# Gates of two hidden-layer units computed as Exp, add, reciprocal and product instead of Silu

## The chip, the cores and the metric

The program runs on one core of a Trainium2 chip. The time is the device time of one execution in microseconds (us); 678.58 us is the median of three runs (678.49 to 678.67). Engines are named as in the profile: PE multiplies matrices (PEld loads its weights), DVE is the vector engine, ACT the scalar engine that evaluates functions from tables, POOL the general engine, SP the queue that starts most transfers.

## The reference

Attention with a sliding window and sink keys, then two feed-forward layers, all in float32. Inputs are 2 batches of 768 tokens, 8 heads of 64, so 1536 tokens of width 512.

```python
scores = scale * np.matmul(q, k.transpose(0, 1, 3, 2))      # q, k, v: (2, 8, 768, 64)
keep = is_sink | in_window                                  # 4 sink keys, window 128
a = np.exp(scores - max);  a = a / (sum(a) + 1e-09);  x = a @ v
g = x @ w_gate                                              # (1536, 512) @ (512, 1536)
silu = g * (1.0 / (1.0 + np.exp(-g)))
y = (silu * (x @ w_val)) @ w_out
h = y @ w_in                                                # 512 -> 2048
out = (np.maximum(h, 0) + alpha * np.minimum(h, 0)) @ w_out2
```

## The kernel before

Tokens are cut into three passes of 512 (`b` = 0, 1, 2). Every float32 product is made of three matmuls of split operands (high by high, low by high, high by low), so a 128x512 projection tile is 12 matmuls (L613 to L615). Weights come as 64-bit numbers; a `Stream` turns them into high and low halves: a copy on ACT (L520), three DVE steps (`w_m`: L536, L539, L542), a copy `wh` on ACT (L550) and a subtraction `wl` (L557, on POOL during attention, on DVE later).

**Attention.** 24 groups of two query blocks and two heads go through a software pipeline (`attention`, L322). In step x group x gets its scores (PE L217; DVE L221 and L223; ACT Exp into `pr`, L227), group x-1 its normalisation (DVE L243 and L244, POOL L259 and L260), group x-3 its product with v (PE L313 and L316 into `xp`; ACT `xh` L805; DVE `xl` L806) and group x-2 its transposes (PE L272, L295; ACT L283, L296; POOL L284, L288).

**Two units woven in.** Once the 512 tokens of a pass are through attention, the first unit of the first layer for that pass, `m1.unit(0, b)`, is taken up piece by piece between attention's steps (`product`, L819). That happens for `b` = 0 and `b` = 1; the third pass and all later chunks run behind attention in `mix`. A unit has four hidden tiles, in two pairs: two gate projections `pg`, a gate `sg` for each (L656, L657), two value projections `pv`, the product `hid` (DVE L665), its halves `hh` (ACT L626) and `hl` (DVE L627). Then the four tiles go through the output projection `po`.

**What sets the order.** During attention the DVE instructions stand in the order in which the program writes them (`manual_schedule`, L799); on the other engines a scheduler sets the order when the program is built. Each engine then runs its list in order. All PSUM tiles, `pg` among them, come from one pool of eight buffers (L865), so a new tile waits until an earlier one has been read for the last time.

**Tables.** [...] Before an Exp (L227) that follows a Silu (L657), and before a Silu that follows an Exp, the built program holds an ACT_TABLE_LOAD. Copy and Abs need none here.

Of the kernel before, what the change touches and what calls it, by code (L numbers as in the profile page):

```python
# [11 lines left out]
AF = mybir.ActivationFunctionType  # L12
ALU = mybir.AluOpType
# [459 lines left out]
def new_acc(g, name):  # L473
    for pool in g.acc_ps:
        if pool[1]:
            pool[1] -= 1
            return pool[0].tile([P, KD, T], F32, tag="acc", name=name), pool
    assert False


def big(g, dt, name):
    return g.x_p.tile([P, KD, T], dt, tag="x", name=name)
# [126 lines left out]
def proj(nc, ps, w, xh, xl):  # L609
    wh, wl = w  # L610
    for kk in range(KD):
        c = slice(kk * P, (kk + 1) * P)
        nc.tensor.matmul(ps, wh[:, c], xh[:, kk], start=(kk == 0), stop=False)  # L613
        nc.tensor.matmul(ps, wh[:, c], xl[:, kk], start=False, stop=False)  # L614
        nc.tensor.matmul(ps, wl[:, c], xh[:, kk], start=False, stop=(kk == KD - 1))  # L615
# [5 lines left out]
def hidden_pair(g):  # L621
    return [g.h_p.tile([P, 2, T], F32R, tag=t, name=t) for t in ("hh", "hl")]


def split_hidden(nc, hid, hh, hl):
    nc.scalar.activation(hh, hid, AF.Copy)  # L626
    nc.vector.tensor_tensor(out=hl, in0=hid, in1=hh, op=ALU.subtract)  # L627


class Moe1:  # L630
# [4 lines left out]
    def unit(self, c, b):  # L635
        nc, g, st = self.nc, self.g, self.st
        nch = NF1 // CHUNK
        w0 = self.base + c * 3 * CHUNK

        def at(kind, x):  # L640
            return w0 + 2 * (x - x % 2) + 2 * kind + x % 2

        xh, xl = self.xs[b]
        last = b == len(self.xs) - 1
        hid_of = []
        for x in range(0, CHUNK, 2):
            pair = hidden_pair(g)
            pss, sgs = [], []
            for r in range(2):
                ps = g.ps_m.tile([P, 512], F32, tag="ps", name="pg")  # L650
                proj(nc, ps, st.get(at(0, x + r)), xh, xl)
                pss.append(ps)
                if r == 0:
                    yield
            for ps in pss:
                sg = g.t_p.tile([P, T], F32, tag="sg", name="sg")  # L656
                nc.scalar.activation(sg, ps, AF.Silu)  # L657
                sgs.append(sg)
            yield
            for r in range(2):  # L660
                hh, hl = (t[:, r] for t in pair)
                ps = g.ps_m.tile([P, 512], F32, tag="ps", name="pv")
                proj(nc, ps, st.get(at(1, x + r)), xh, xl)
                hid = g.t_p.tile([P, T], F32, tag="hid", name="hid")
                nc.vector.tensor_tensor(out=hid, in0=ps, in1=sgs[r], op=ALU.mult)  # L665
                split_hidden(nc, hid, hh, hl)
                hid_of.append((hh, hl))
                if last and r == 1:
                    st.done(4)
                yield  # L670
        if c == 0:
            self.accs[b] = new_acc(g, "acc1")
        acc, home = self.accs[b]
        if c == nch - 1:
            yh, yl = big(g, F32R, "yh"), big(g, F32R, "yl")
        for m in range(KD):
            mc = slice(m * P, (m + 1) * P)
            ps = g.ps_m.tile([P, 512], F32, tag="ps", name="po")
            for x, (hh, hl) in enumerate(hid_of):
                wh, wl = st.get(w0 + 2 * CHUNK + x)  # L680
                nc.tensor.matmul(ps, wh[:, mc], hh, start=(x == 0), stop=False)  # L681
                nc.tensor.matmul(ps, wl[:, mc], hh, start=False, stop=False)  # L682
                nc.tensor.matmul(ps, wh[:, mc], hl, start=False, stop=(x == CHUNK - 1))  # L683
            av = acc[:, m]
            if c == 0:
                nc.scalar.activation(av, ps, AF.Copy)
            else:
                nc.vector.tensor_tensor(out=av, in0=ps, in1=av, op=ALU.add)
            if c == nch - 1:
                split_hidden(nc, av, yh[:, m], yl[:, m])  # L690
            yield
        if c == nch - 1:
            home[1] += 1
            self.put(yh, yl)
        if last:
            st.done(CHUNK)
# [241 lines left out]
```

## Time and profile before

| | |
|---|---|
| median of 3 runs | 678.58 us |
| the profiled execution | 679.03 us, span 677.3 us |
| PE busy | 656.8 us, 97% of the span |
| DVE busy | 395.5 us, 58% |
| ACT busy | 297.4 us, 44% |
| POOL busy | 82.7 us, 12% |
| mean granted PE clock | 0.983 of full speed |

The span is what the profiler saw; the execution's own time is 1.7 us longer. The page cuts the span into 40 slices of 16.9 us and gives the busy share of each engine and the granted PE clock in tenths. In a list of groups each line has the busy time, the mean duration of one instruction, and the idle time of the engine in front of it with the instruction that ended it. In a timeline a bracket after a row is idle time of that engine just before the row, and what ended it. The first unit that is woven in has its gates at 57 to 85 us, the second at 127 to 155 us; the last Exp of attention is at 163 us.

### The profile page before, as it was taken

Reading aid. Unit: us, or ns where it says so; the run is one execution under the profiler, and the core shown is the slowest. Engines: PE = TensorE matmul, PEld = TensorE weight load, DVE = VectorE, ACT = ScalarE, POOL = GpSimd, SP = SyncE. Lnnn points to the kernel's source line nnn. Section 1 sums busy time; section 2 is a strip of 40 time slices with the busy share of each in tenths; the row PEclk is TensorE's granted clock in tenths of the full one; section 3 lists DMA queues with packets and bytes.
Section 4 is the critical chain, followed back from the end, with each engine's and each line's share of the span. In section 5 each row is a group of like instructions: output and inputs, shape, how many; then the busy total and the mean of one; then the engine's idle time right before and its main releaser. Section 6 shows DMA issues by size and latency. Waiting matters only on the chain.

```text
span 677.3 us, 8596 instructions
## 1 busy us (share of the span) xinstructions
PE 656.8 (97%) x3098; PEld 520.0 (77%) x3098; DVE 395.5 (58%) x880; ACT 297.4 (44%) x680; POOL 82.7 (12%) x137
## 2 busy tenths in 40 slices
PE   7789899999999999999999999999999999999996
PEld 4457566767788888888888888888888888888885
DVE  6997867353389923389332789419734744334332
ACT  4767756765476612255221546336522333112320
POOL 3557544334100000000000000000000000000000
PEclk8969799999999999999999999999999999999999
DMA  8854444100055510045200134203400000000111
GB/s 274 259 158 136 146 135 145 31 13 1 1 180 168 180 63 1 4 124 180 65 1 0 39 118 133 84 1 95 154 1 0 1 1 0 1 0 8 55 63 67
DMA packets 37203, 52.29 MB, mean 77 GB/s; under 512 B 4384, under 2 KB 28960, under 8 KB 37152
## 3 DMA queue, kind: packets, MB, share of 16 engines
q1 hardware_dynamic: 34944, 51.65, 24.0%
q8 instruction: 26, 0.43, 0.3%
q10 hardware_dynamic: 2208, 0.01, 0.2%
q14 instruction: 25, 0.20, 0.1%
HBM read 48.51 MB, written 3.15 MB: 76 GB/s over the span
## 4 chain that ended last, share of the span: by engine, by line
PE 86%; DVE 6%; ACT 3%; DMA 1%; issue 1%; POOL 1%; SPq 0%; ACTq 0%; POOLq 0%
PE ph L613 6%; PE ph L615 6%; PE pf L739 6%; PE pf L737 6%; PE pf L738 6%; PE ph L614 6%; PE po L681 5%; PE po L682 5%; PE po L683 5%; PE pv L613 5%; PE pv L615 5%; PE pv L614 5%; PE pg L613 5%; PE pg L614 4%; PE pg L615 4%; PE ps_s L217 2%
## 5 line engine op out<-in xcount | busy, mean ns | idle before, releaser
L626 ACT ACTIVATE hh<-hid 128x512 fp32r<-128x512 f32 x84 | 53.0, 632 | 69.6 <-DVE hid L665 40.2
L627 DVE TENSOR_TENSOR hl<-hid,hh 128x512 fp32r<-128x512 f32 x84 | 58.2, 693 | 35.8 <-ACT hh L626 35.6
L613 PE MATMUL ph<-yh,wh 128*128 128x512 f32 x192 | 74.8, 390 | 0.0
L615 PE MATMUL ph<-yh,wl 128*128 128x512 f32 x192 | 74.8, 389 | 0.0
L738 PE MATMUL pf<-wl,hh 128*128 128x512 f32 x192 | 74.7, 389 | 0.0
L614 PE MATMUL ph<-yl,wh 128*128 128x512 f32 x192 | 74.7, 389 | 0.0
L737 PE MATMUL pf<-wh,hh 128*128 128x512 f32 x192 | 74.7, 389 | 0.0
L719 ACT ACTIVATE neg<-ph,sal 128x512 f32<-128x512 f32 x48 | 33.0, 687 | 93.0 <-PE ph L615 93.0
L739 PE MATMUL pf<-wh,hl 128*128 128x512 f32 x192 | 72.1, 389 | 0.0
L550 ACT ACTIVATE wh<-w_m 128x512 fp32r<-128x512 f32 x68 | 42.6, 630 | 64.6 <-DVE w_m L542 23.4
L721 DVE SCALAR_TENSOR_TENSOR hid<-ph,sig,neg 128x512 f32<-128x512 f32 x48 | 36.0, 750 | 38.2 <-ACT neg L719 38.0
L613 PE MATMUL pg<-xh,wh 128*128 128x512 f32 x144 | 57.9, 403 | 0.0
L613 PE MATMUL pv<-xh,wh 128*128 128x512 f32 x144 | 56.9, 395 | 0.3 <-ACT pt L283 0.3
L614 PE MATMUL pg<-xl,wh 128*128 128x512 f32 x144 | 57.2, 397 | 0.0
L615 PE MATMUL pg<-xh,wl 128*128 128x512 f32 x144 | 56.9, 395 | 0.0
L681 PE MATMUL po<-hh,wh 128*128 128x512 f32 x144 | 56.6, 395 | 0.2 <-ACT pr L227 0.2
L615 PE MATMUL pv<-xh,wl 128*128 128x512 f32 x144 | 56.1, 390 | 0.0
L614 PE MATMUL pv<-xl,wh 128*128 128x512 f32 x144 | 56.1, 389 | 0.0
L682 PE MATMUL po<-hh,wl 128*128 128x512 f32 x144 | 55.9, 390 | 0.0
L557 DVE TENSOR_TENSOR wl<-w_m,wh 128x512 fp32r<-128x512 f32 x56 | 38.3, 688 | 27.9 <-ACT wh L550 27.9
L744 DVE TENSOR_TENSOR acc<-pf,acc 128x512 f32<-128x512 f32 x36 | 23.2, 686 | 52.0 <-PE pf L739 52.0
L683 PE MATMUL po<-hl,wh 128*128 128x512 f32 x144 | 52.9, 390 | 0.0
(106 smaller groups left out, 1203.8 us busy)
## 6 DMA issues: line engine op xcount, KB each, us to landing
w_raw<-in_moe_w_out SPq DMA_DIRECT2D x28, 512.0 KB, 3.5
w_raw<-in_moe_w_in SPq DMA_DIRECT2D x16, 512.0 KB, 3.8
w_raw<-in_moe_w_gate SPq DMA_DIRECT2D x12, 512.0 KB, 4.4
w_raw<-in_moe_w_val SPq DMA_DIRECT2D x12, 512.0 KB, 3.9
th<-in_qk SPq DMA_DIRECT2D x16, 336.0 KB, 3.3
vr<-in_v SPq DMA_DIRECT2D x16, 192.0 KB, 2.6
out<-acc SPq DMA_DIRECT2D x12, 256.0 KB, 2.2
th<-in_qk SPq DMA_DIRECT2D x8, 256.0 KB, 5.3
```

The costliest lines, as they stand in the source:

```text
L550: nc.scalar.activation(wh, m, AF.Copy)
L613: nc.tensor.matmul(ps, wh[:, c], xh[:, kk], start=(kk == 0), stop=False)
L614: nc.tensor.matmul(ps, wh[:, c], xl[:, kk], start=False, stop=False)
L615: nc.tensor.matmul(ps, wl[:, c], xh[:, kk], start=False, stop=(kk == KD - 1))
L626: nc.scalar.activation(hh, hid, AF.Copy)
L627: nc.vector.tensor_tensor(out=hl, in0=hid, in1=hh, op=ALU.subtract)
L681: nc.tensor.matmul(ps, wh[:, mc], hh, start=(x == 0), stop=False)
L682: nc.tensor.matmul(ps, wl[:, mc], hh, start=False, stop=False)
L683: nc.tensor.matmul(ps, wh[:, mc], hl, start=False, stop=(x == CHUNK - 1))
L737: nc.tensor.matmul(ps, hh[:, ts], wh, start=(x == 0), stop=False)
L738: nc.tensor.matmul(ps, hh[:, ts], wl, start=False, stop=False)
L739: nc.tensor.matmul(ps, hl[:, ts], wh, start=False, stop=(x == CHUNK - 1))
```

## The change

For the first chunk (`c == 0`) of the first two passes (`b < 2`), which are the two units woven into attention, the gate g * 1/(1 + exp(-g)) is written out: Exp with scale -1 on ACT, then on DVE an addition of 1, a reciprocal and the product with `pg`. All other gates keep Silu. Eight gates change, four in each unit. Lines behind L657 move down by six.

```diff
             for ps in pss:
                 sg = g.t_p.tile([P, T], F32, tag="sg", name="sg")
-                nc.scalar.activation(sg, ps, AF.Silu)
+                if c == 0 and b < 2:
+                    nc.scalar.activation(sg, ps, AF.Exp, scale=-1.0)
+                    nc.vector.tensor_scalar(out=sg, in0=sg, scalar1=1.0, scalar2=None, op0=ALU.add)
+                    nc.vector.reciprocal(out=sg, in_=sg)
+                    nc.vector.tensor_tensor(out=sg, in0=ps, in1=sg, op=ALU.mult)
+                else:
+                    nc.scalar.activation(sg, ps, AF.Silu)
                 sgs.append(sg)
```

On DVE this is the list around the first pair of gates (at 55 us of the trace), before:

```order
177 L243 TENSOR_SCALAR rinv<-ssum 128x4
178 L244 RECIPROCAL rinv<-rinv 128x4
179 L536 TENSOR_SCALAR w_m<-w_m 128x512
180 L539 SCALAR_TENSOR_TENSOR w_m<-w_raw,w_m 128x512
181 L542 SCALAR_TENSOR_TENSOR w_m<-w_raw,w_m 128x512
182 L806 TENSOR_TENSOR xl<-xp,xh 128x256
183 L221 COPY_PREDICATED ps_s<-above,ps_s 128x128
```

The same place in the changed kernel's DVE list:

```order
177 L243 TENSOR_SCALAR rinv<-ssum 128x4
178 L244 RECIPROCAL rinv<-rinv 128x4
179 L659 TENSOR_SCALAR sg<-sg 128x512
180 L660 RECIPROCAL sg<-sg 128x512
181 L661 TENSOR_TENSOR sg<-pg,sg 128x512
182 L659 TENSOR_SCALAR sg<-sg 128x512
183 L660 RECIPROCAL sg<-sg 128x512
184 L661 TENSOR_TENSOR sg<-pg,sg 128x512
185 L536 TENSOR_SCALAR w_m<-w_m 128x512
186 L539 SCALAR_TENSOR_TENSOR w_m<-w_raw,w_m 128x512
187 L542 SCALAR_TENSOR_TENSOR w_m<-w_raw,w_m 128x512
188 L812 TENSOR_TENSOR xl<-xp,xh 128x256
```

The six gate steps stand ahead of a weight's conversion, of `xl` and of the next group's scores. The other three pairs are inserted in the same way, each right behind a normalisation; the rest of the DVE list in attention stays, but for a few neighbours that change places.

On ACT, at the same pair, before:

```order
60 L227 ACTIVATE pr,ssum<-ps_s,nb 128x160
61 L657 ACT_TABLE_LOAD
62 L657 ACTIVATE sg<-pg 128x512 x2
63 L550 ACTIVATE wh<-w_m 128x512
64 L805 ACTIVATE xh<-xp 128x256
65 L283 ACTIVATE pt<-ps_p 128x2x128 x2
66 L296 ACTIVATE pts<-ps_p_792 128x128
67 L520 ACTIVATE w_m,wsum<-w_raw 128x512
68 L227 ACT_TABLE_LOAD
69 L227 ACTIVATE pr,ssum<-ps_s,nb 128x160 x4
```

And after:

```order
60 L227 ACTIVATE pr,ssum<-ps_s,nb 128x160
61 L658 ACTIVATE sg<-pg 128x512 x2
62 L811 ACTIVATE xh<-xp 128x256
63 L283 ACTIVATE pt<-ps_p 128x2x128 x2
64 L296 ACTIVATE pts<-ps_p_798 128x128
65 L811 ACTIVATE xh<-xp 128x256
66 L283 ACTIVATE pt<-ps_p 128x2x128 x2
67 L550 ACTIVATE wh<-w_m 128x512
```

Both loads are gone, `xh` moves up and `wh` moves down behind the next group's copies. In the part of the list that runs with these inputs 16 loads become two: one for the first Exp and one for the first Silu behind attention.

The PE list keeps the order of its blocks (projections, scores, products, transposes). What changes is what they wait for. Between the two value projections of the first pair, with the semaphores waited for in brackets, before:

```order
163 L272 MATMUL ps_p<-ident,pr 128x128 [waits Activation_49]
164 L272 MATMUL ps_p<-ident,pr 128x128
165 L272 MATMUL ps_p<-ident,pr 128x128 [waits Activation_49]
166 L313 MATMUL xp<-pt,vr 64x128 [waits Pool_49]
167 L313 MATMUL xp<-pt,vr 64x128
168 L316 MATMUL xp<-pts,vsr 128x128 x2
169 L272 MATMUL ps_p<-ident,pr 128x128
170 L295 MATMUL ps_p_881<-ident,sk 128x128 [waits Activation_49]
171 L613 MATMUL pv<-xh,wh 128x512 [waits Activation_49]
```

And after:

```order
163 L313 MATMUL xp<-pt,vr 64x128 [waits Pool_49]
164 L313 MATMUL xp<-pt,vr 64x128
165 L316 MATMUL xp<-pts,vsr 128x128 x2
166 L272 MATMUL ps_p<-ident,pr 128x128 [waits DVE_49]
167 L272 MATMUL ps_p<-ident,pr 128x128
168 L272 MATMUL ps_p<-ident,pr 128x128 [waits Activation_49]
169 L272 MATMUL ps_p<-ident,pr 128x128
170 L295 MATMUL ps_p_887<-ident,sk 128x128 [waits Activation_49]
171 L613 MATMUL pv<-xh,wh 128x512 [waits DVE_49]
```

The transposes at row 166 take over the buffer of the pair's second `pg`, which is now read last by DVE's product (L661) and no longer by ACT; the projection at row 171 takes the buffer of the `xp` behind it and waits for DVE's `xl`.

## Rows read from the trace of the kernel before

**Rows 1.** The page: busy time of PE and DVE, the PE slices, the granted clock.
```profile
PE 656.8 (97%) x3098; PEld 520.0 (77%) x3098; DVE 395.5 (58%) x880; ACT 297.4 (44%) x680; POOL 82.7 (12%) x137
...
PE   7789899999999999999999999999999999999996
...
PEclk8969799999999999999999999999999999999999
```

**Rows 2.** Windows: length, busy time by engine (instructions), granted clock, DMA share, GB/s.
```profile
55.10:103.10 48.00, 44.08 (x243) 30.59 (x241) 36.15 (x100) 32.32 (x88) 26.05 (x36) 0.93 0.47 147
79.00:91.00 12.00, 12.00 (x55) 8.35 (x54) 5.55 (x12) 8.24 (x22) 6.39 (x10) 0.78 0.45 141
103.10:126.40 23.30, 23.09 (x128) 16.51 (x129) 14.49 (x64) 13.92 (x50) 10.46 (x19) 1.00 0.31 104
126.40:162.00 35.60, 34.77 (x202) 25.03 (x202) 15.76 (x66) 24.75 (x59) 11.52 (x24) 1.00 0.04 12
```

**Rows 3.** Groups of ACT: table loads and gates; busy us, mean ns, idle before.
```profile
L657 ACT ACTIVATE sg<-pg 128x512 f32<-128x512 f32 x36 | 21.2, 594 | 37.5 <-PE pg L615 37.4
...
L227 ACT ACT_TABLE_LOAD x8 | 10.3, 1283 | 3.7 <-DVE nb L223 1.9 <-PEq L922 1.7
L657 ACT ACT_TABLE_LOAD x8 | 10.3, 1283 | 0.1
```

**Rows 4.** Timeline of PE from 74 to 88 us: start, us, engine, instruction, idle before.
```profile
74.32 0.33 PE L295 MATMUL ps_p<-ident,sk 128*128 128x128 f32 x1 [0.37 <-ACT sg L657]
76.11 1.54 PE L217 MATMUL ps_s<-th 64*128 64x288 f32 x6 [1.47 <-ACT pr L227]
78.05 1.33 PE L217 MATMUL ps_s<-th 64*128 64x288 f32 x2 [0.40 <-ACT pt L283]
...
79.90 0.63 PE L614 MATMUL pg<-xl,wh 128*128 128x512 f32 x1
80.33 0.63 PE L615 MATMUL pg<-xh,wl 128*128 128x512 f32 x1
...
87.41 0.39 PE L615 MATMUL pv<-xh,wl 128*128 128x512 f32 x1
87.64 0.40 PE L613 MATMUL pv<-xh,wh 128*128 128x512 f32 x1
```

**Rows 5.** Timeline of ACT and DVE around the first two gates.
```profile
55.03 0.18 DVE L244 RECIPROCAL rinv<-rinv 128x4 f32<-128x4 f32 x1
...
55.95 1.28 ACT L657 ACT_TABLE_LOAD   x1
...
59.16 0.42 DVE L806 TENSOR_TENSOR xl<-xp,xh 128x256 fp32r<-128x256 f32 x1 [1.38 <-ACT xh L805]
```

**Rows 6.** Waits of DVE from 55.1 to 103.1 us: total us, times, longest.
```profile
DVE xl L806 <- ACT xh L805: 5.7, 2, 4.3
DVE hl L627 <- ACT hh L626: 2.9, 3, 1.3
DVE hid L665 <- PE pv L615: 1.8, 2, 1.6
```

**Rows 7.** Groups of DVE: the kinds of operation that the change adds, at several sizes.
```profile
L665 DVE TENSOR_TENSOR hid<-pv,sg 128x512 f32<-128x512 f32 x36 | 24.7, 687 | 44.7 <-PE pv L615 43.6 <-ACT sg L657 1.0
...
L531 DVE TENSOR_SCALAR w_m<-w_m 128x512 f32<-128x512 f32 x16 | 6.8, 423 | 0.7 <-ACT w_m L518 0.6
...
L100 DVE TENSOR_TENSOR sal<-alpha,sig 128x16 f32<-128x16 f32 x1 | 0.2, 175 | 0.0
...
L144 DVE TENSOR_SCALAR red<-lim_v 128x1 f32<-128x1 f32 x1 | 0.1, 143 | 0.0
```

**Rows 8.** The reciprocal's own line: duration in ns, least, median and greatest.
```profile
L244 DVE RECIPROCAL rinv<-rinv x24: 169/178/179, 10.5 to 165.2; 128x4 f32<-128x4 f32 x24
```

**Rows 9.** Timeline of DVE and PE at 69 us, and where both meet again.
```profile
69.16 0.74 DVE L627 TENSOR_TENSOR hl<-hid,hh 128x512 fp32r<-128x512 f32 x1 [0.70 <-ACT hh L626]
...
103.14 0.42 DVE L806 TENSOR_TENSOR xl<-xp,xh 128x256 fp32r<-128x256 f32 x1
...
103.61 0.44 PE L272 MATMUL ps_p<-ident,pr 128*128 128x128 f32 x2
```

**Rows 10.** Timeline of PE in the second unit: its only wait.
```profile
148.81 0.75 PE L217 MATMUL ps_s<-th 64*128 64x288 f32 x2 [0.83 <-ACT pr L227]
```

**Rows 11.** Waits of DVE from 126.4 to 162 us.
```profile
DVE xl L806 <- ACT xh L805: 11.9, 3, 5.7
DVE hid L665 <- PE pv L615: 5.2, 3, 2.5
```

## The prediction

> **What bounds the kernel now.** I read the page first: PE is busy 656.8 of 677.3 us, and its slices show that what it loses lies in the first sixth of the span, where the granted clock is also below full [rows 1]. Behind attention every slice is 9, so the change, which adds nothing there, can move the time only through the attention stage. Next I read that stage by windows around the two units woven in [rows 2]. From 55.10 to 103.10 us (48.00 us, the first unit's gates) PE is busy 44.08 us at a clock of 0.93, and DVE 36.15 us. From 126.40 to 162.00 us (35.60 us, the second unit's gates) PE is busy 34.77 us at full clock, DVE only 15.76 us. So the first unit sits where PE and DVE are both near full, the second where PE alone bounds.
>
> Then the groups of ACT show the price of alternating functions: 8 loads before a Silu and 8 before an Exp, 1283 ns each, 20.6 us in all [rows 3]. The timeline shows what part of that reaches PE. [...] In the second unit a load costs PE one wait of 0.83 us [rows 10]. Last I read DVE's waits in the first unit: 5.7 us for `xh`, late behind a load, 2.9 us for `hh`, 1.8 us for `pv` [rows 6].
>
> **The change part by part.**
>
> *Loads on ACT.* Sixteen become two; 14 x 1.283 = 18.0 us of ACT work goes. The eight Exp take the place of eight Silu of the same shape, 0.594 us [rows 3]; Exp itself at 128x512 is not in the trace, and I take the same. ACT bounds nothing for long (32.32 of 48.00 us in the first unit [rows 2]), so this is worth only what PE and DVE waited: on PE 0.37 + 1.47 + 0.40 = 2.24 us and the low clock behind it, twelve matmuls x (0.43 - 0.23) = 2.4 us [rows 4], and 0.83 us in the second unit [rows 10]; 5.5 us at the very best.
>
> *Three DVE steps for each of eight gates.* The addition is like the 128x512 TENSOR_SCALAR on float32 at L531, 0.423 us; the product from PSUM is like `hid`, 0.687 us [rows 7]. The reciprocal of 128x512 is not in the trace; that of 128x4 takes 178 ns [rows 8]. The nearest rows to scale it with are TENSOR_TENSOR at 16 and 512 elements, 175 and 687 ns [rows 7]: (687 - 175)/496 = 1.03 ns per element and a fixed part of 175 - 16 x 1.03 = 158 ns. Four elements at that rate would take 162 ns. The reciprocal takes 178, so (178 - 158)/4 = 5 ns per element, and 512 elements take 0.158 + 512 x 0.005 = 2.7 us. The lower bound is the ordinary rate, 0.69 us, if the 16 ns more are only a longer fixed part. The upper bound takes the fixed part from the one-element row, 143 ns [rows 7]: 35/4 = 8.75 ns per element, 4.6 us. I take 2.7 us, because it rests on the rows closest to it in kind. A gate then costs DVE 0.42 + 2.7 + 0.69 = 3.8 us, four gates 15.2 us.
>
> *What is queued behind them.* DVE runs in written order. In the first pair the gates stand ahead of a weight's conversion, `xl` and the next scores. DVE is free at 55.03 + 0.18 = 55.21 us; Exp can start where the load started, at 55.95 [rows 5], and ends 0.6 us later, so DVE first waits 1.35 us. The second pair stands behind scores and a normalisation; by then PE has its `pg` ready, and I count no wait. PE's transposes, products and `pv` now wait for L661 and for the `xl` behind it. Scores on ACT and POOL's normalisation move with DVE. The DMA queues get nothing new: the conversion that is pushed back belongs to weights that are needed two blocks later.
>
> *The sum for the first unit.* In the 48.00 us DVE has 36.15 us of work [rows 2]. Added: 15.2 us for the gates. Waits that remain: 1.35 us for the first Exp and three times 0.70 us, which is what `hl` waits for `hh` with no load in the way [rows 9], 2.1 us. The waits for `xh` and `pv` [rows 6] go, because DVE is now the late one. 36.15 + 15.2 + 1.35 + 2.1 = 54.8 us, 6.8 us more than 48.00. PE can't run ahead of that: at 103.61 us it starts transposes directly behind DVE's `xl` of 103.14 [rows 9], and after 103.10 DVE has little slack until PE bounds again (PE 23.09 of 23.30 us [rows 2]). So PE arrives 6.8 us later. Its own old waits and the low clock lie inside those 54.8 us and give nothing back. PE will now idle more in this stretch, and the rows show a low clock after such waits [rows 4]; where that falls at the end of the stretch it costs PE time, 2.4 us a time. I take half of one, 1.2 us.
>
> *The second unit.* Four gates are 15.2 us of DVE; DVE is idle 35.60 - 15.76 = 19.8 us there [rows 2], 11.9 us of it waiting for `xh` and 5.2 us for `pv` [rows 11]. This cover holds them, and PE's wait of 0.83 us goes: -0.8 us. If the reciprocal took 4.6 us, four gates would be 22.9 us and 3.1 us would show.
>
> *Together:* 679.03 + 6.8 + 1.2 - 0.8 = 686.2 us for an execution like the profiled one. That one lies 0.45 us above the median of 678.58, so 685.8 us.
>
> **The rivals.**
>
> *The reciprocal is slower still.* For: the four-element row allows 8.75 ns per element. Against: with the fixed part of the tensor operations it allows 5. At 4.6 us a gate costs 5.7 us, the first unit 36.15 + 22.9 + 3.45 = 62.5 us, 14.5 us more; the second unit shows 3.1 - 0.8 us more; 695.4 us against the median. [...] I give this rival 0.15.
>
> *The clock falls more.* Each further stretch at the lower level that ends in PE's own time costs 2.4 us [rows 4]; two more give 690 to 691 us. Chance 0.10.
>
> *Faster: the loads were what held PE, and DVE keeps up.* If the reciprocal runs at the ordinary rate of 0.69 us, a gate is 1.8 us, and the first unit takes 36.15 + 7.2 + 3.45 = 46.8 us, 1.2 us less than before; with the second unit's 0.83 us that is 676.6 us. If PE is then held by nothing it reaches -5.5 us, 673.1 us. The point from which this decides: four gates must cost less than 48.00 - 36.15 - 3.45 = 8.4 us, a reciprocal below 1.0 us. For it: the loads' waits are real [rows 4]. [...] Against it: the 178 ns. Chance 0.16.
>
> *No change.* A reciprocal between 1.0 and 1.7 us, or the two groups of lag in attention's pipeline, swallow the delay. The lag would do so only if PE had other work ready, but PE's list is fixed and waits for DVE's `xl` in it. Chance 0.12.
>
> **How the numbers follow.** The forecast itself, a delay of DVE in the first unit at 2 to 3.6 us per reciprocal, has 0.47, and its own range is 682 to 690 us. With the slower reciprocal and the lower clock, slower has 0.47 + 0.15 + 0.10 = 0.72. What counts as no change is 0.2% or 1.4 us, about what a measurement of this kernel can tell: 677.2 to 679.9 us, 0.12. Faster has 0.16. The range that should hold 8 of 10 goes from 676.2 us, which takes in the ordinary-rate case, to 696 us, the upper bound of the reciprocal; left out are the full 5.5 us gain below, and more clock loss on top of the upper bound.
>
> **What would show it.** Two table loads instead of sixteen, and none between 55 and 160 us. RECIPROCAL at L660: 2.7 us; under 1 us or over 4 us would make the forecast wrong by its step. In the first unit DVE busy nearly throughout, with no wait for `xh`, and its stretch from the norm ahead of the first gate to the `xl` that stood at 103.14 us some 55 us long. PE with new waits for L661 (`sg`), for `xl` (L812) and for `pr`, in place of those for ACT between loads. In the second unit PE without a wait for `sg`. If the stretch is longer by the gates' 15 us, the old waits were not there to be filled; if PE waits in the second unit too, its cover was read too generously.

## The result, and the profile after

The changed kernel takes 688.10 us (median of 4 runs, 687.07 to 689.14) against 678.62 us of the kernel before; the ratio is 1.014, with an interval of 1.0127 to 1.0153. It is slower by some 9.5 us. The forecast was 685.8 us, slower, in a range of 676.2 to 696.0.

The page of the changed kernel, answering to [rows 1]: busy time, PE's slices, the granted clock.

```profile
PE 660.7 (96%) x3098; PEld 521.7 (76%) x3098; DVE 426.3 (62%) x904; ACT 280.7 (41%) x666; POOL 83.0 (12%) x137
...
PE   7878988999999999999999999999999999999996
...
PEclk8889897999999999999999999999999999999998
```

ACT has 16.7 us less to do, DVE 30.8 us more, and PE's losses still lie in the first sixth of the span. The groups of the gates' steps answer to [rows 3, 7, 8] (busy us, mean ns, idle before):

```profile
L660 DVE RECIPROCAL sg<-sg 128x512 f32<-128x512 f32 x8 | 26.8, 3353 | 0.3
...
L661 DVE TENSOR_TENSOR sg<-pg,sg 128x512 f32<-128x512 f32 x8 | 5.5, 691 | 0.3
L658 ACT ACTIVATE sg<-pg 128x512 f32<-128x512 f32 x8 | 4.6, 595 | 2.2 <-PE pg L615 2.2
...
L659 DVE TENSOR_SCALAR sg<-sg 128x512 f32<-128x512 f32 x8 | 4.2, 530 | 1.6 <-ACT sg L658 1.6
L227 ACT ACT_TABLE_LOAD x1 | 1.3, 1283 | 1.7 <-PEq L928 1.7
L663 ACT ACT_TABLE_LOAD x1 | 1.3, 1283 | 0.0
```

Two loads are left of sixteen. Exp takes what Silu took (595 and 594 ns a gate). The reciprocal takes 3.353 us every time.

To see where the time went I cut both traces at the same three instructions, so that the same work lies between them: L244's norm ahead of the first gate, the fifth norm behind it (the first unit's gates lie between these), and the first `pg` behind attention. The windows of before (length, busy time by engine, clock, DMA share, GB/s):

```profile
55.03:106.10 51.07, 46.94 (x256) 32.67 (x255) 39.05 (x115) 35.17 (x98) 28.18 (x40) 0.93 0.49 152
106.10:181.24 75.14, 74.31 (x440) 53.97 (x438) 30.99 (x124) 43.77 (x123) 27.06 (x56) 1.00 0.09 29
```

And of the changed kernel:

```profile
55.62:115.42 59.80, 50.36 (x256) 34.73 (x255) 54.44 (x128) 28.28 (x92) 26.77 (x37) 0.86 0.40 126
115.42:191.32 75.90, 75.16 (x444) 54.30 (x442) 48.34 (x136) 33.89 (x115) 28.79 (x58) 1.00 0.10 29
```

Of the profiled difference of 10.0 us (span 687.3 against 677.3), 0.6 us is there at the first norm, ahead of every changed instruction. That is the spread of runs: in the profiles below this norm lies anywhere from 53.8 to 55.9 us, so I compare lengths from there. The first unit is 8.7 us longer, the rest of attention 0.8 us, and nothing is added behind it. In the first unit DVE is busy 54.44 of 59.80 us. Its timeline answers to [rows 5] (start, us, engine, instruction, idle before):

```profile
57.16 0.47 DVE L659 TENSOR_SCALAR sg<-sg 128x512 f32<-128x512 f32 x1 [1.35 <-ACT sg L658]
57.66 3.35 DVE L660 RECIPROCAL sg<-sg 128x512 f32<-128x512 f32 x1
61.05 0.69 DVE L661 TENSOR_TENSOR sg<-pg,sg 128x512 f32<-128x512 f32 x1
61.66 0.42 DVE L659 TENSOR_SCALAR sg<-sg 128x512 f32<-128x512 f32 x1
62.11 3.35 DVE L660 RECIPROCAL sg<-sg 128x512 f32<-128x512 f32 x1
65.50 0.69 DVE L661 TENSOR_TENSOR sg<-pg,sg 128x512 f32<-128x512 f32 x1
...
68.04 0.41 DVE L812 TENSOR_TENSOR xl<-xp,xh 128x256 fp32r<-128x256 f32 x1
```

From 57.16 to 68.04 us DVE never waits, and `xl`, which waited 1.38 us for ACT before [rows 5], now stands behind two gates. The waits of PE in the first unit follow from that; those for L661 and `xl` are direct. The longest, 4.20 us for `pr` up to 105.78 us, comes by way of DVE: the Exp on ACT that ends it waited 0.98 us for the scores' last step on DVE (`nb`, L223). The other waits for `pr` I read in the same way, without having followed each. Total us, times, longest:

```profile
PE ps_s L217 <- ACT pr L227: 4.5, 2, 4.2
PE ps_p L295 <- ACT pr L227: 1.4, 1, 1.4
PE ps_p L272 <- DVE sg L661: 1.3, 1, 1.3
...
PE ps_p L272 <- DVE xl L812: 0.3, 1, 0.3
```

The Exp and the scores of that longest wait, from the timeline:

```profile
105.24 0.39 ACT L227 ACTIVATE pr<-ps_s,nb 128x160 f32<-128x160 f32 x1 [0.98 <-DVE nb L223]
105.78 2.37 PE L217 MATMUL ps_s<-th 64*128 64x288 f32 x4 [4.20 <-ACT pr L227]
```

### The profile page after: what moved, and what is told of

It is laid out like the page before. It is cut to its first block, busy times and chain, and to the rows that moved or that the text cites. A ratio compares the mean times of both kernels' runs of the same rounds, so it can differ in the third digit from the quotient of the medians.

```text
span 687.3 us, 8599 instructions
## 1 busy us (share of the span) xinstructions
PE 660.7 (96%) x3098; PEld 521.7 (76%) x3098; DVE 426.3 (62%) x904; ACT 280.7 (41%) x666; POOL 83.0 (12%) x137
## 4 chain that ended last, share of the span: by engine, by line
PE 88%; DVE 5%; ACT 2%; issue 2%; POOL 1%; DMA 1%; SPq 0%; ACTq 0%; POOLq 0%
PE ph L614 6%; PE ph L615 6%; PE pf L744 6%; PE pf L745 6%; PE pf L743 6%; PE ph L613 6%; PE po L687 5%; PE po L688 5%; PE po L689 5%; PE pg L613 5%; PE pv L613 5%; PE pg L614 5%; PE pg L615 5%; PE pv L615 4%; PE pv L614 4%; PE xp L313 3%
## 5 line engine op out<-in xcount | busy, mean ns | idle before, releaser
L615 PE MATMUL pg<-xh,wl 128*128 128x512 f32 x144 | 56.5, 393 | 0.0
L688 PE MATMUL po<-hh,wl 128*128 128x512 f32 x144 | 56.5, 395 | 0.0
```

## The experiments

Theory 1: the gates' time on DVE, three quarters of it the reciprocal, delays the first unit, where DVE was nearly full; the second unit has room for it. The rivals: both units lose; PE is held because DVE's product is now the last reader of `pg`'s PSUM buffers; the order of the list is what costs; the loads were worth little. Most edits below also make the scheduler put some instructions of ACT and POOL in another order, so that more than the edited line differs.

**One unit at a time.** The first unit alone:

```diff
-                if c == 0 and b < 2:
+                if c == 0 and b == 0:
```

> The four steps stand in the first unit only; the second unit's gates are Silu again, with a load before each Silu and each Exp there. Theory 1 (DVE's time for the gates, mostly the 3.35 us reciprocal, delays the first unit alone): 687 to 689 us, and the stretch from the first gate's norm to the xl behind the second pair about 56.5 us as in the changed kernel. Rival (the loss is shared by both units, 5 us each): 683 us. Rival (the order of the whole list, not the place): the same as the changed kernel, but then the second unit alone would lose as well.

And the second alone:

```diff
-                if c == 0 and b < 2:
+                if c == 0 and b == 1:
```

> The four steps stand in the second unit only; the first unit is that of the kernel before, with its loads. Theory 1: the second unit's idle DVE time holds four gates of 4.44 us (17.8 of 19.8 us), and the wait of 0.83 us goes: 677.8 to 679 us, no change that can be measured. Rival (the loss is shared by both units): 683 us. The stretch of the first unit should be 48.1 us as before.

Measured: 688.68 us (ratio 1.0149, 1.013 to 1.0169) and 678.21 us (0.9999, 0.9989 to 1.0009). The whole loss is in the first unit, and the rival of an equal share falls. With the first unit alone changed, its windows are 59.79 and 75.69 us long, those of the changed kernel within 0.3 us. The run with the second unit alone also tells the spread of such windows: its first unit, where the source is that of before, is 49.90 us long against 51.07.

**Without the reciprocal.** The same list, with a cheap step in its place:

```diff
-                    nc.vector.reciprocal(out=sg, in_=sg)
+                    nc.vector.tensor_scalar(out=sg, in0=sg, scalar1=1.0, scalar2=None, op0=ALU.mult)
```

> A multiplication by 1.0 (0.42 us) stands in place of each reciprocal, so the gate leaves out the inverse: it is g times (1 + exp(-g)). Order, buffers and loads are those of the changed kernel. Theory 1: a gate costs DVE 1.5 us, the first unit 36.15 + 6.1 + 3.45 = 45.7 us, and with the second unit's 0.83 us the time is 675 to 677 us, faster than before. Rival (the product on DVE holds the two PSUM buffers of pg and changes the order, whatever it lasts): still 683 us or more. Rival (the loads were worth nothing): 678.6 us.

Measured: 678.23 us (1.0000, 0.9988 to 1.0012), 1.2 us above the upper end of what I expected. DVE's list is that of the changed kernel but for the step itself and a few neighbours that change places, while some copies and Exp of ACT and steps of POOL are in another order. So the 9.9 us between this and the changed kernel are the reciprocals, together with what that order is worth. That the steps cost 9 us by their place in DVE's list or by being the last readers of `pg`, however short they are, falls here. That a hold of `pg` which lasts 3.35 us longer costs something does not; it is taken up below. That the time only comes back to that of before, with fourteen loads gone, means that the other steps eat what the loads had cost: the stand-in took 0.65 us in the first unit and not 0.42, the addition 0.50, and a gate 1.84 us in place of the 1.5 I had put in.

**Gates from Tanh.** The same function is g/2 * (1 + tanh(g/2)), which needs one DVE step a gate; the half goes into the step that makes `hid`:

```diff
-                    nc.scalar.activation(sg, ps, AF.Exp, scale=-1.0)
-                    nc.vector.tensor_scalar(out=sg, in0=sg, scalar1=1.0, scalar2=None, op0=ALU.add)
-                    nc.vector.reciprocal(out=sg, in_=sg)
-                    nc.vector.tensor_tensor(out=sg, in0=ps, in1=sg, op=ALU.mult)
+                    nc.scalar.activation(sg, ps, AF.Tanh, scale=0.5)
+                    nc.vector.scalar_tensor_tensor(out=sg, in0=sg, scalar=1.0, in1=ps, op0=ALU.add, op1=ALU.mult)
...
+                if c == 0 and b < 2:
+                    nc.vector.scalar_tensor_tensor(out=hid, in0=ps, scalar=0.5, in1=sgs[r], op0=ALU.mult, op1=ALU.mult)
...
```

> The gate is made with ACT's Tanh of half the argument and one DVE step, (t + 1) times pg; the factor 0.5 goes into the step that makes hid. No reciprocal, no sum of its own. Theory 1: four gates cost DVE about 0.7 us each, 2.8 us a unit, and the loads are gone if Tanh needs no other table than Exp: 673 to 676 us, faster than both. If Tanh needs a table of its own there are 16 loads again and the time is 679 to 682 us. Rival (holding pg's buffer until DVE's step is what costs): 683 us or more.

Measured: 671.02 us (0.9895, 0.9878 to 0.9913), faster than both kernels and beyond what I expected. Its groups show two loads of 1.283 us, one at the first Exp (L227) and one at the first Silu behind attention (L661), so Tanh needed none beside Exp's here, and one DVE step of 0.68 us. Its two windows:

```profile
54.77:99.97 45.20, 43.22 (x258) 30.77 (x257) 39.39 (x118) 27.80 (x92) 29.68 (x40) 1.00 0.53 169
99.97:172.87 72.90, 72.90 (x440) 53.40 (x438) 33.89 (x128) 34.06 (x115) 27.16 (x56) 1.00 0.10 31
```

PE has the full clock throughout and waits 2.0 us in the first unit, none behind it.

**The loads alone, and both together.** What the removed loads were worth by themselves:

```diff
-                nc.scalar.activation(sg, ps, AF.Silu)
+                nc.scalar.activation(sg, ps, (AF.Exp if (c == 0 and b < 2) else AF.Silu))
```

> The kernel before with Exp in place of Silu in the two units and nothing on DVE, so the gate is exp(g) and the rest of its formula is left out. This is the loads' removal alone. If DVE's sum bounds the first unit down to this point, its stretch is 36.15 + 2.1 = 38.3 us against 42.25 us of the tanh gates, and the time 667 us; if PE bounds it from about 42 us on, the stretch stays at 42 us and the time at 670 to 671 us, as the tanh gates. If the loads were worth no more than the 5.5 us of the forecast's best case: 673 us.

And the opposite corner, all loads kept and DVE's steps added:

```diff
                 nc.scalar.activation(sg, ps, AF.Silu)
+                if c == 0 and b < 2:
+                    dm = g.t_p.tile([P, T], F32, tag="hid", name="dm")
+                    nc.vector.tensor_scalar(out=dm, in0=sg, scalar1=1.0, scalar2=None, op0=ALU.add)
+                    nc.vector.reciprocal(out=dm, in_=dm)
+                    nc.vector.tensor_tensor(out=dm, in0=ps, in1=dm, op=ALU.mult)
```

> The kernel before with its Silu gates and all 16 loads, to which the three DVE steps (addition, reciprocal, product with pg) are added on a scratch tile that nothing else reads. Set against the changed kernel this is the loads alone, at the same DVE work. Theory 1a (DVE bounds the first unit with the gates in it, and the loads' waits lie inside, as the forecast had it): 688 to 690 us, as the changed kernel. Theory 1b (the loads stand on the same chain as DVE's steps, since the tanh gates brought 7.4 us): 6 to 8 us more than the changed kernel, 694 to 696 us. Rival (DVE's steps cost nothing themselves, the gates' order does): 679 to 681 us.

Measured: 670.95 us (0.9904, 0.9886 to 0.9922) and 700.63 us (1.0333, 1.0316 to 1.0350). The first of these kernels runs the lists of the kernel before, engine by engine, with nothing but 14 loads taken out. So the loads were worth 7.3 us by themselves, and DVE's steps cost 17.2 us on top of their removal (688.10 - 670.95); the change is the difference. The Tanh kernel ends where the loads' removal alone does: its DVE steps cost nothing that the times show. With DVE's steps in place the loads cost 12.5 us, more than either branch of my expectation allowed. The windows say where. Loads alone removed:

```profile
53.83:99.47 45.64, 43.79 (x254) 30.82 (x253) 38.05 (x115) 27.46 (x92) 28.85 (x40) 0.96 0.53 169
99.47:172.73 73.26, 73.26 (x442) 53.70 (x440) 31.42 (x124) 34.41 (x116) 26.77 (x56) 1.00 0.09 30
```

Loads and steps together:

```profile
54.51:119.96 65.45, 51.95 (x252) 35.49 (x251) 54.27 (x127) 35.49 (x98) 26.17 (x37) 0.82 0.37 118
119.96:204.86 84.90, 79.45 (x442) 57.06 (x441) 47.23 (x136) 43.99 (x124) 29.93 (x58) 0.96 0.09 26
```

In the first unit the two add up, as far as single executions tell (the one with both took 2.0 us more than the median of its runs): 45.64 us with neither, 5.4 us more with the loads, 14.2 us more with the steps, 19.8 us more with both. Behind it they don't: 73.26 us with neither, 1.9 us more with the loads, 2.6 with the steps, 11.6 with both. The second unit can hide either one and not the two in a row; PE's waits there with both are for ACT (`pr`, `pt`, 5.4 us in all), and the rest is PE at a granted clock of 0.96 in place of 1.00.

**Who holds pg.** A buffer of `pg` comes free after its last reader, which in the change is DVE's product (PE's transposes waited 1.3 us for it, above). If the product reads another tile in its place, ACT is the last reader again and the number of DVE steps stays the same. First with Silu and the loads (the line shown differs from the kernel just above), then in the changed kernel:

```diff
-                    nc.vector.tensor_tensor(out=dm, in0=ps, in1=dm, op=ALU.mult)
+                    nc.vector.tensor_tensor(out=dm, in0=sg, in1=dm, op=ALU.mult)
```

> As the run with Silu and the three steps, but the product reads the finished gate in place of pg, so ACT is the last reader of pg's PSUM buffers and nothing of PE waits for these steps directly. Theory 1 (DVE's time): the same as that run within 1 us. Rival (PE is held by pg's buffers until the product, not by DVE's time): 3 us or more below it, near 681 to 686 us.

```diff
-                    nc.vector.tensor_tensor(out=sg, in0=ps, in1=sg, op=ALU.mult)
+                    nc.vector.tensor_tensor(out=sg, in0=sg, in1=sg, op=ALU.mult)
```

> The changed kernel, but the product reads the gate's reciprocal twice and not pg, so the factor g is left out; DVE does the same number of steps of the same size, and ACT is the last reader of pg's PSUM buffers. With Silu and its loads in place the same edit took 2.7 us off. If holding pg costs the changed kernel as much: 685.4 us, and PE's waits for L661 before transposes and projections are gone. If DVE's time alone decides, as PE waits for the xl behind the gates anyway: 687 to 689 us, with the wait moved to xl.

Measured: 697.90 us, 2.7 us below the run that holds `pg` and so between the two branches that I had expected, and 689.17 us (1.016, 1.0143 to 1.0177), no less than the changed kernel. So in the change itself the buffers cost nothing. Its waits show why:

```profile
PE ps_s L217 <- ACT pr L227: 5.6, 3, 2.8
PE ps_p L272 <- DVE xl L812: 2.2, 1, 2.2
```

The wait for L661 is gone, and in its place PE waits for the `xl` that stands behind the same gates; its waits for `pr` come to 5.9 us in either kernel. With the loads the hold costs something, all of it in the first unit (65.45 against 61.68 us). There DVE itself stands idle once, for 4.32 us, ahead of `hl`, for ACT's `hh`. Without the hold DVE waits 0.70 us at this place. Whether `hh` is late there by PE's wait of 2.4 us for the product, by the lower clock (0.82 in that unit against 0.86) or by the other order is not shown.

**More of it, in either unit.** The reciprocal done twice, in the first unit or in the second:

```diff
                     nc.vector.reciprocal(out=sg, in_=sg)
+                    if b == 0:
+                        nc.vector.reciprocal(out=sg, in_=sg)
```

> The changed kernel with the reciprocal done twice in the first unit, which leaves the inverse out there: 4 x 3.35 = 13.4 us more of DVE. If DVE bounds the first unit, each us shows in full: 688.1 + 13.4 = 701.5 us, or up to 704 us with a lower clock behind longer waits of PE. If part of the loss was the loads, the order or pg's buffers and not DVE's time, less: under 697 us.

```diff
                     nc.vector.reciprocal(out=sg, in_=sg)
+                    if b == 1:
+                        nc.vector.reciprocal(out=sg, in_=sg)
```

> The changed kernel with the reciprocal done twice in the second unit, which leaves the inverse out there. Its four gates cost DVE 4 x 7.8 = 31.2 us there, against 19.8 us that it had idle. Theory 1 (the second unit hides what fits into DVE's idle time, and no more): 688.1 + 11.4 = 699.5 us, or down to 694 us if the gates' waits overlap with DVE's work ahead of them. Rival (the second unit is never held by DVE, because PE has other work ready): 688 us. Rival (each added us costs there as in the first unit): 688.1 + 13.4 = 701.5 us.

Measured: 701.50 us (1.0347, 1.0326 to 1.0368) and 704.02 us (1.0386, 1.0369 to 1.0403). In the first unit 13.4 us of DVE cost 13.4 us. Here DVE's list is that of the changed kernel with four reciprocals added, and PE's differs only in the place of two transposes, so little besides DVE's time can have moved it. In the second they cost 15.9 us, beyond every expectation: the room there was already used up by the change. The waits of PE from 114.59 us on, in the kernel with the second unit doubled:

```profile
PE ps_p L272 <- DVE sg L663: 6.1, 1, 6.1
PE xp L313 <- issue: 5.4, 2, 4.9
PE pv L613 <- DVE sg L663: 1.2, 1, 1.2
```

The profile names no releaser for the 4.9 us ahead of `xp`; this wait ends at 184.11 us, 0.1 us behind the pair's second product (L663, 183.32 to 184.01 us). In either pair the two added reciprocals are 6.7 us, and PE waits about 6 us (6.1, and 1.2 + 4.9); the low clock behind these waits (0.94 over that stretch, PE busy 78.21 us against 75.16) is the other 3 us:

```profile
114.59:205.73 91.14, 78.21 (x444) 57.05 (x442) 62.20 (x140) 33.80 (x115) 28.92 (x58) 0.94 0.09 25
```

Together the runs give the first unit as a function of what the gates cost DVE in it (sums of the steps' busy time in its window). The windows not yet shown are those without the reciprocal and with it doubled:

```profile
54.64:104.90 50.26, 45.58 (x254) 32.24 (x253) 44.44 (x127) 27.31 (x92) 28.08 (x40) 0.93 0.48 156
54.75:127.84 73.09, 53.14 (x251) 35.95 (x252) 67.78 (x132) 27.96 (x92) 25.88 (x37) 0.79 0.35 106
```

| gates' DVE time, us | 0 (loads removed only) | 2.6 (Tanh) | 7.4 (no reciprocal) | 17.9 (the change) | 31.4 (doubled) |
|---|---|---|---|---|---|
| first unit, us | 45.64 | 45.20 | 50.26 | 59.80 | 73.09 |

It is flat to about 2.6 us, where PE bounds (busy 43.22 of 45.20 us), and then rises by 1.07, 0.91 and 0.99 us per us.

**Later, and in halves.** The three steps one stage later in the list, behind `xl` and the scores; the Exp stays where it is (against the kernel before):

```diff
...
+            if c == 0 and b < 2:
+                for ps, sg in zip(pss, sgs):
+                    nc.vector.tensor_scalar(out=sg, in0=sg, scalar1=1.0, scalar2=None, op0=ALU.add)
+                    nc.vector.reciprocal(out=sg, in_=sg)
+                    nc.vector.tensor_tensor(out=sg, in0=ps, in1=sg, op=ALU.mult)
             for r in range(2):
```

> The changed kernel with the three DVE steps of a pair moved one stage later in the woven list, behind the weight's conversion, xl and the scores that they stood ahead of, and before hid, which needs them. Same steps, same number. If DVE's total in the first unit decides: 687 to 690 us. If what decides is that PE's next work (xl, scores) stands queued behind 8.9 us of gates: 3 us or more less, 683 to 685 us. If pg's buffers decide, held longer now: more than 690 us.

Measured: 693.94 us (1.0234, 1.0208 to 1.0261), 5.8 us worse. The first unit is 61.05 us long, 1.3 us more than in the changed kernel, and the rest 81.38 us against 75.90. There, PE's longest wait is a new one, a projection for `pg`'s buffer:

```profile
PE pg L613 <- DVE sg L667: 2.2, 1, 2.2
```

All waits of PE there come to 4.8 us against 0.7, and the rest is clock (0.98). Over both units PE waits 7.3 us for the late product, against 1.3 us in the changed kernel, so the branch in which a longer hold of `pg` costs is the one that came in. The place ahead of `xl` was not what cost: leaving it brought none of the 3 us expected from it. As I read it, gates directly ahead of `hid` lose the time in which PE had other work; the hold and that reading are not told apart.

```diff
-                    nc.vector.reciprocal(out=sg, in_=sg)
+                    nc.vector.reciprocal(out=sg[:, :256], in_=sg[:, :256])
+                    nc.vector.reciprocal(out=sg[:, 256:], in_=sg[:, 256:])
```

> The changed kernel with each reciprocal cut into two of 128x256. From 178 ns at 4 elements and 3.353 us at 512 the line is 6.25 ns per element and a fixed 153 ns, so a half takes 1.75 us and two 3.51 us. If the price is not linear in the elements, a half departs from 1.75 us. The time is that of the changed kernel within 1.5 us.

One run gave 689.09 us. The first halves show the line's price to a nanosecond (least, median, greatest); the second halves, which follow at once, 1.695 us:

```profile
L660 DVE RECIPROCAL sg<-sg x8: 1752/1752/1754, 57.7 to 165.9; 128x256 f32<-128x256 f32 x8
```

## Why the prediction was right, and which of its terms were off

The mechanism and the sign were right: DVE's added time in the first unit is the loss, PE follows it, and the second unit hides its gates. The time came out 2.3 us above the forecast. Between the profiled executions, forecast 686.2 us and measured 689.14, the first unit is 8.7 us longer (forecast 6.8 + 1.2), what follows it 0.8 us longer (forecast 0.8 shorter), and 0.6 us is there ahead of the change. By its steps:

*The reciprocal* was put at 2.7 us and takes 3.353 us. The term was mis-sized in its fixed part: 178 ns at 4 elements and 3353 ns at 512 give 6.25 ns per element and a fixed 153 ns, where I took 158 ns from tensor operations. Five ns of fixed part, spread over four elements and carried to 512, became 0.65 us. Four gates cost 17.9 us in the first unit and not 15.2.

*The first unit's sum.* From the norm to the `xl` that stood at 103.14 us [rows 9] I expected 54.8 us. In the changed kernel, from the norm's end to that `xl`, now at 112.14 us:

```profile
55.69:112.10 56.41, 46.97 (x232) 32.12 (x230) 51.22 (x112) 25.57 (x82) 25.50 (x36) 0.86 0.38 119
```

It has the 100 instructions of before [rows 2] and twelve of the gates. The hundred leave 51.22 - 17.89 = 33.3 us of busy time and not 36.15, which offsets the dearer reciprocal. DVE waits 2.4 us for `hh` and 1.4 us for the first Exp (2.1 and 1.35 expected), never for `xh`. The other 1.4 us are small gaps between DVE's instructions; they were as large before (48.00 less 36.15 busy and 10.4 of waits [rows 2, 6]), and the sum had no term for them. That two errors of nearly 3 us offset each other was luck: nothing in the prediction said that the old steps would take less.

*The low clock behind new waits* was a term of 1.2 us at the end of the unit. In the kernel before the granted clock is 0.50 from 79.00 to 84.00 us, behind PE's waits, and 1.00 from 86.00 us. In the change it did fall further, from 0.93 to 0.86 in the first unit, but behind it PE is at 1.00 at once, and with the reciprocal doubled the clock is 0.79 there while the unit grows by no more than DVE's time. So the slower PE cost nothing of its own in this stretch, which DVE bounds. The term was not there. The delay stayed to the end for the reason given, that PE is full behind it; that DVE had little slack after 103.10 us was misread, since it is busy 14.49 of 23.30 us there [rows 2].

*The second unit* was put at -0.8 us and came out at +0.8 (75.14 to 75.90 us with all that follows), as the sum of -1.9 for the loads and +2.6 for DVE's steps. Its cover held, with next to nothing left, as the doubled reciprocal shows: counting the idle 19.8 us as one pool [rows 11] was near the truth only because the gates' 18.7 us there (2.5 + 13.4 + 2.8) still fitted.

*The loads* I put at 5.5 us at the very best; alone they are worth 7.3. In the first unit PE's waits fall from 51.07 - 46.94 = 4.1 us to 1.9, and its busy time for the same work from 46.94 to 43.79 us. I had counted the low clock at one stretch, 2.4 us; over the whole unit it was 3.2 us. This did not enter the sum, which was built from DVE's work.

*The rivals.* The reciprocal at the upper bound did not occur; the clock fell further but cost no time of its own. For the faster case, at an ordinary rate, I gave 676.6 us; the run with an ordinary step in that place took 678.23, so the three steps alone were enough to undo the loads' gain. That attention's lag swallows the delay is ruled out by the slope of one.

*What was to show it.* Two loads; L660 between 1 and 4 us; DVE without a wait for `xh`; a stretch of 56.5 us where I said 55; PE with new waits for L661, `xl` and `pr`, and none for `sg` in the second unit: all seen.

## What to carry to other kernels

Work moved to another engine is priced in the stretch where that engine is near full. In the first unit each us showed in full (0.91 to 1.07 us); in the second the gates' 18.7 us cost 2.6 us, and with the room gone 13.4 us more cost 15.9. That room has to be counted between two points where the other engine waits. Two costs that a stretch hides one by one need not be hidden together (1.9 and 2.6 us alone, 11.6 together), so test them together. To save table loads, look first for a form of the function that adds none to those in place: Tanh with one DVE step gave 671.02 us, where Exp with three gave 688.10.

## What the runs showed of the hardware

A reciprocal on DVE took 6.25 ns per element on 128 partitions (0.178, 1.752 and 3.353 us at 4, 256 and 512), six times the 1.03 ns worked out from TENSOR_TENSOR on float32 [rows 7].

The same DVE instruction took longer beside some work of POOL; why is not shown: L539, 128x512, takes 1.39 to 1.41 us in the kernel before, the five times that it starts within POOL's L259 between 55 and 113 us, and 0.69 to 0.77 us the other four times. The first of them:

```profile
55.35 1.06 POOL L259 TENSOR_TENSOR pr<-pr,rinv 128x512 f32<-128x512 f32 x1 [0.84 <-DVE rinv L244]
...
55.56 1.41 DVE L539 SCALAR_TENSOR_TENSOR w_m<-w_raw,w_m 128x512 int32<-128x512 int32 x1
```

The gates separated these two in the changed kernel: its eight L539 in that stretch take 0.711 us on the mean, against 1.069 before, 2.9 us in all. That is the largest part of the shrinking of the hundred old steps above, and not the whole account: L542 takes 1.0 us more in all (one of them 1.41 us beside the L259 at 82.84 us), `hl` takes 0.6 us more, L243 0.6 us less. The durations of the old steps add up to 1.8 us less; the other 1.0 us of the 2.8 comes from counting, as the records of DVE overlap at their ends (the L661 above that starts at 61.05 us lasts 0.69 us, and the next step starts at 61.66). The reciprocal does not change beside POOL: 3.353 us in all eight cases, two of them beside an L259 (from 88.25 and 161.48 us). The addition takes 0.40 us at the least and 1.22 at most; the longest starts at 136.92 us, 0.1 us behind the start of an L259.
